# Keys and queries loaded once, both heads' scores side by side on 64 rows, one transfer to turn the results

## The chip, the core and the metric

The kernel runs on one core of a Trainium2 chip. The metric is the device time of one execution in microseconds (us). Before the change three runs took 953.39, 953.75 and 956.28 us, median 953.75. The engines are named as in the profile: PE (matrix products; PEld is its weight load), DVE (vector), ACT (scalar), POOL (GpSimd), and SP, which here only issues transfers (DMA).

## What is computed

Attention with a window and global keys, then a two-layer MLP with the Mish function, on its output read as tokens. `d` is 64, there are 8 batches and 8 heads, 512 local and 32 global positions, and the MLP maps 4608 tokens of 512 to 2048 and back.

```python
s_g = scale * q_g @ [k_g, k_l]^T                  # 32 global queries see all 544 keys
out_g = softmax(s_g) @ [v_g, v_l]
s_l = scale * [q_l @ k_g^T, q_l @ k_l^T where |i - j| <= 32]
out_l = softmax(s_l) @ [v_g, v_l]
x = concat([out_g, out_l]) as (4608, 512) tokens
h = x @ w_in                                      # (512, 2048)
g = h * tanh(softplus(h))
return g @ w_out                                  # (2048, 512)
```

## The kernel before, in words

**Tiles.** Two heads form a head pair, and a batch `b` has four of them (`hp`). A head pair's 512 local queries are four tiles `t` of 128. A tile sees a window of 192 or 224 key columns, in which the 32 global keys stand (`WIN`). One (b, hp, t) is a *unit*; there are 128. The tokens of a batch make two MLP blocks of 256, and the global tokens of all batches a seventeenth. A block passes eight *steps*: each step takes 256 of the 2048 hidden columns through `m1_mm` (product `h`, line 915), `mish` (ACT, line 958), `g_hi`/`g_lo` (split into two fp16 parts) and `m2_mm` (product `o`, line 983).

**Precision.** An fp32 operand is split into a high part and a remainder, both fp16, and a product is made of three fp16 products (high by high, high by low, low by high). The weights come in 64-bit words, which DVE takes apart (`w_bits`, `w_sum`) slice by slice, before a statistic over the whole matrix (`w_stat` on PE, `w_norm`, line 463) gives the scale with which `w_split` splits them. So the first `h` needs all of the first matrix, and the first `o` all of the second.

**Scores.** For the first eight head pairs (batches 0 and 1, `plain_s`) scores are fp32 products over 64 rows, one per head, line 692. For the other 24 the keys and queries lie twice in a tile of 128 rows: both row halves of `kraw` and of `qraw` hold the same head's 64 numbers, the two heads one behind the other in the columns. `q_hi` writes the high part over all 128 rows of `qs`, `q_lo` puts the remainder over its upper 64, `k_hi` and `k_lo` make `ks` and `kl`. One product of `qs` by `ks` over 128 rows thus holds two of the terms, and a second by `kl` the third (line 699). Each tile and head has a PSUM bank of its own from the ring "sc" of three, read by `row_max` (DVE, line 705); `expo` (ACT, line 714) follows, then `p_hi`, `p_lo` (`ph`), a DMA transpose into `pt`, and `pv` (product `U`, line 783). `g_scores` (line 823) does the global queries with 32 columns of weights for each head, its two parts in two more banks of "sc".

**Results.** `x_norm` divides, `x_split` makes two fp16 parts in `xs`, and `x_turn` turns them with two DMA transposes into `xh` and `xl`, from which `m1_mm` reads. In batch 0 PE turns `pt` and `x` instead.

**Order.** Nothing is issued as it is written. `Plan.add` records each piece of work with what it reads and writes, an engine (or two to choose from) and a cost in ns; `Plan.order` is a list scheduler over these costs, and `emit` writes the engines' instructions in its order. Each engine runs them in that order, and all transfers go through SP. `slot(u)` is the order of priority in which pieces are added for unit u; `ORDER`, `CONV1` and the other constants set where the first loads and the work on the weights come. In the stretch before PE has enough to do, the planner adds *fillers*: products of a constant into `w_s` (line 1211) that nothing reads.

Of the kernel before, what the change touches and what calls it, by code (L numbers as in the profile page):

```python
# [39 lines left out]
NPS = 8  # L40
# [11 lines left out]
class Plan:  # L52
# [10 lines left out]
    SLACK = 357.177  # L63
    TARGET = 6095.107
    SPARE_T = 129630.527
    BOOST = 0.15
    SPARE = 1463.76
    TABLE = 1283

    def __init__(self):  # L70
        self.tasks = []
        self.rings = {}
        self.count = {}
        self.last = {}
# [7 lines left out]
        self.fill, self.filler = {}, None  # L82

# [17 lines left out]
    def add(self, eng, ns, fn, r=(), w=(), new=(), pri=0, rows=1.0, table=None):  # L101
# [14 lines left out]
        for tag, name in new:  # L116
            bufs, make = self.rings[tag]
            k = (tag, self.count[tag] % bufs)
            self.count[tag] += 1
            for wr, rd in self.state.get(k, {}).values():  # L120
                deps |= rd
                if wr is not None:
                    deps.add(wr)
# [5 lines left out]
            self.state[k] = {None: (n, set())}  # L129
        for x in w:  # L130
            k, sub = self._key(x)
            st = self.state.setdefault(k, {})
            for s, (wr, rd) in st.items():
# [112 lines left out]
def attn_mish_kernel(ctx: ExitStack, tc: tile.TileContext, qt, kt, qt0, kt0, mxs, vm, vg, qg, w1, w2, consts_in, out, w64):  # L246
# [23 lines left out]
    def rings(pool, *table):  # L270
        for tag, bufs, shape, dt in table:
# [5 lines left out]
          ("vraw", 1, [128, HP, 4, 128], F32), ("vgraw", 1, [128, 128], F32), ("qgraw", 1, [128, 3, HP, 64], F32),  # L277
# [14 lines left out]
          ("xh", 2, [128, HP, SL], F16), ("xl", 2, [128, HP, SL], F16),  # L292
# [32 lines left out]
    def dma(kib):  # L325
        return 410, kib * 3.05
# [4 lines left out]
    def dma_on(kib):  # L331
        return 590, 250 + kib * 4.5
# [52 lines left out]
    PLACE = dict(zip(range(16), ["xh", "xl"] * 2 + list(range(9, 18)) + ["G"] * 3))  # L385
    PLACE.update(zip(range(16, 32), ["G"] * 3 + [17, 16, 15, 14, "kraw", "qraw", "ob", 17, 16, "kraw", "qraw", "ob", 8]))

    def raw(k):
# [13 lines left out]
    def w_load(k):  # L402
# [11 lines left out]
        if w64:  # L414
            p = PLACE[k]
            pl.add(DMA, bulk(512), go, w=[rawkey(k)] if p in range(18) else (), new=() if p in range(18) else [(p, ("wraw", k))])
# [175 lines left out]
    def g_split(b):  # L592

        q, rq, sk = ("qgh", b), ("qgraw", b), ("sk", b)
        pl.add([(ACT, act(512, 1)), (DVE, dve2(512, 1))], 0, lambda e: scaled(e, X[q], X[rq][:, 1:3], X[sk][:, 0:1]), r=[rq, sk], new=[("qgh", q)])
        for a, h in ((0, HI), (1, LO)):
            pl.add(DVE, dve(256, 1), lambda a=a, h=h: V.scalar_tensor_tensor(X[q][h, a], X[rq][h, 1 + a], X[sk][h, 0:1], X[q][h, a], ALU.mult,
                                                                          ALU.subtract), r=[rq, sk], w=[[q, a]])
# [22 lines left out]
    def q_hi(b, hp):  # L621
        q, qs = ("qraw", b, hp), ("qs", b, hp)
        pl.add(COPY(1024, b), 0, lambda e: scaled(e, X[qs], X[q], X["sk", b][:, 0:1]), r=[q, ("sk", b)], new=[("qs", qs)])

    def q_lo(b, hp):

        q, qs = ("qraw", b, hp), ("qs", b, hp)
        pl.add(DVE, dve(1024, 1) + 90, lambda: V.scalar_tensor_tensor(X[qs][HI], X[q][HI], X["sk", b][HI, 0:1], X[qs][HI], ALU.mult, ALU.subtract),
               r=[q, ("sk", b)], w=[qs])

    def k_hi(b, hp):
        k, ks = ("kraw", b, hp), ("ks", b, hp)
        pl.add(COPY(1280, b), 0, lambda e: scaled(e, X[ks], X[k], X["sk", b][:, 1:2]), r=[k, ("sk", b)], new=[("ks", ks)])

    def k_lo(b, hp, h):
        k, ks, kl = ("kraw", b, hp), ("ks", b, hp), ("kl", b, hp)
        pl.add(DVE, dve(640, 1), lambda: V.scalar_tensor_tensor(X[kl][:, h], X[k][:, h], X["sk", b][:, 1:2], X[ks][:, h], ALU.mult, ALU.subtract),  # L637
               r=[k, ks, ("sk", b)], w=[[kl, h]], new=() if h else [("kl", kl)])
# [46 lines left out]
    def scores(b, hp, t, h):  # L685
        qs, ks, kl, s = ("qs", b, hp), ("ks", b, hp), ("kl", b, hp), ("s", b, hp, t, h)
        c0, w, m0 = WIN[t]
        r = slice(h * 64, h * 64 + 64)

        if plain_s(b, hp):  # L690
            (q, part), (k, _) = pair(b, hp, "qn"), pair(b, hp, "kn")
            pl.add(PE, mm(1, 4 * w) + 50, lambda: T.matmul(X[s][:, :w], X[q][r, part, t * 128:(t + 1) * 128],
# [605 lines left out]
```

## Time and profile before

| | us |
|---|---|
| runs, median | 953.75 |
| profiled execution, device time | 956.89 |
| its span, first to last instruction | 955.1 |
| ACT busy | 640.0 |
| read from HBM | 75.15 MB |
| granted TensorE clock, mean | 0.985 |

An engine's busy time is the union of its instructions, and a matmul's row shows it from its start to the modelled end, so that rows of matmuls overlap: what one costs is the distance between starts. `x103` counts instructions. A row of waits gives the idle time in total, how often, and the longest. The views that the prediction rests on are shown there.

### The profile page before, as it was taken

Reading aid. Unit: us, or ns where it says so; the run is one execution under the profiler, and the core shown is the slowest. Engines: PE = TensorE matmul, PEld = TensorE weight load, DVE = VectorE, ACT = ScalarE, POOL = GpSimd, SP = SyncE. Lnnn points to the kernel's source line nnn. Section 1 sums busy time; section 2 is a strip of 40 time slices with the busy share of each in tenths; the row PEclk is TensorE's granted clock in tenths of the full one; section 3 lists DMA queues with packets and bytes.
Section 4 is the critical chain, followed back from the end, with each engine's and each line's share of the span. In section 5 each row is a group of like instructions: output and inputs, shape, how many; then the busy total and the mean of one; then the engine's idle time right before and its main releaser. Section 6 shows DMA issues by size and latency. Waiting matters only on the chain.

```text
span 955.1 us, 20897 instructions
## 1 busy us (share of the span) xinstructions
PE 919.5 (96%) x8115; PEld 634.9 (66%) x8115; DVE 665.5 (70%) x1775; ACT 640.0 (67%) x1293; POOL 17.6 (2%) x28
## 2 busy tenths in 40 slices
PE   7899999999999999999999999999999999999995
PEld 4566765567676676777767676767777766666663
DVE  6799989779899898767766777768777552322221
ACT  4577778697767889978877887788868771212110
POOL 2000000000000000000000000000000000000000
PEclk8899999999999999999999999999999999999998
DMA  9877458987999896758585676567764430000000
GB/s 303 283 242 234 164 135 204 171 218 193 218 216 255 217 261 150 163 130 185 130 166 118 166 157 148 117 155 166 157 124 102 81 74 12 23 1 23 4 20 22
DMA packets 214011, 141.02 MB, mean 148 GB/s; under 512 B 176664, under 2 KB 188184, under 8 KB 212888
## 3 DMA queue, kind: packets, MB, share of 16 engines
q1 hardware_dynamic: 213912, 139.69, 60.3%
q8 instruction: 63, 1.03, 0.5%
q14 instruction: 36, 0.29, 0.1%
HBM read 75.15 MB, written 8.91 MB: 88 GB/s over the span
## 4 chain that ended last, share of the span: by engine, by line
PE 61%; DVE 19%; ACT 8%; DMA 6%; issue 4%; SPq 1%; POOL 0%; DVEq 0%; ACTq 0%
PE o L983 26%; PE h L915 26%; PE U L783 3%; DMA pt<-ph 2%; PE s L699 2%; DVE G L971 2%; DVE P L705 2%; ACT P L714 2%; ACT L958 2%; DMA vraw<-in_vm 2%; PE g L823 1%; DVE G L351 1%; DVE W L430 1%; ACT e L958 1%; DMA W<-in_w 1%
## 5 line engine op out<-in xcount | busy, mean ns | idle before, releaser
L983 PE MATMUL o<-W,G 128*128 128x512 f16 x1632 | 391.7, 380 | 3.4 <-ACT ob L349 1.3
L915 PE MATMUL h<-xh,W 128*128 128x256 f16 x2048 | 375.9, 273 | 0.9 <-ACT e L958 0.8
L915 PEld LDWEIGHTS <-W 128*128 128x128 f16 x3264 | 311.2, 98 | 66.5 <-issue 6.5
L915 PE MATMUL h<-xl,W 128*128 128x256 f16 x1024 | 279.1, 273 | 0.0
L983 PEld LDWEIGHTS <-G 128*128 128x128 f16 x1632 | 156.8, 98 | 149.3 <-issue 7.7
L958 ACT ACTIVATE e<-h,c 128x512 f32<-128x512 f32 (+1 forms) x137 | 91.5, 682 | 123.8 <-PE h L915 118.4
L351 DVE TENSOR_SCALAR G<-e,c 128x512 f16<-128x512 f32 (+1 forms) x122 | 58.5, 481 | 151.5 <-ACT e L958 151.3
L714 ACT ACTIVATE P<-P,nm 128x192 f32<-128x192 f32 (+1 forms) x256 | 118.0, 461 | 55.1 <-DVE nm L705 52.6
L766 DVE SCALAR_TENSOR_TENSOR ph<-P,ph 128x384 f16<-128x384 f32 (+1 forms) x112 | 65.0, 582 | 57.9 <-ACT ph L349 57.4
L971 DVE SCALAR_TENSOR_TENSOR G<-e,c,G 128x512 f16<-128x512 f32 (+1 forms) x137 | 101.8, 744 | 2.7
L705 DVE CUSTOM_DVE_ANT_0 P<-s,consts 128x192 f32<-128x192 f32 (+1 forms) x256 | 90.9, 362 | 18.2 <-PE s L699 11.4
L958 ACT ACT_TABLE_LOAD x64 | 82.1, 1283 | 1.1
L714 ACT ACT_TABLE_LOAD x60 | 77.0, 1283 | 1.5 <-DVE nm L705 0.4
L783 PEld LDWEIGHTS <-pt 96*128 96x128 f16 (+1 forms) x1536 | 61.5, 98 | 13.2 <-DMA pt<-ph 6.4
L349 ACT ACTIVATE ph<-P 128x384 f16<-128x384 f32 (+1 forms) x111 | 60.2, 547 | 11.8 <-DMA pt<-ph 9.6
L783 PE MATMUL U<-va,pt 128*128 128x64 f16 (+1 forms) x768 | 55.3, 193 | 3.9 <-DMA pt<-ph 3.7
L783 PE MATMUL U<-vc,pt 96*128 96x64 f16 x768 | 55.2, 193 | 0.0
L699 PEld LDWEIGHTS <-qs 128*128 128x128 f16 x384 | 35.3, 98 | 20.7 <-issue 3.4
L714 ACT ACTIVATION_READ_ACCUMULATOR P<-P,nm 128x1 f32 x256 | 47.9, 187 | 0.0
L699 PE MATMUL s<-ks,qs 128*128 128x192 f16 (+1 forms) x192 | 42.6, 253 | 1.5 <-ACT gP L845 0.7
L699 PE MATMUL s<-kl,qs 128*128 128x192 f16 (+1 forms) x192 | 42.5, 252 | 0.0
L637 DVE SCALAR_TENSOR_TENSOR kl<-kraw,sk,ks 128x640 f16<-128x640 f32 x48 | 41.6, 867 | 0.0
(132 smaller groups left out, 935.6 us busy)
## 6 DMA issues: line engine op xcount, KB each, us to landing
kraw<-in_kt SPq DMA_DIRECT2D x24, 640.0 KB, 4.8
kn_m<-in_mxs SPq DMA_DIRECT2D x24, 544.0 KB, 4.8
qraw<-in_qt SPq DMA_DIRECT2D x24, 512.0 KB, 3.4
out<-ob SPq DMA_DIRECT2D x34, 256.0 KB, 2.5
vraw<-in_vm SPq DMA_DIRECT2D x8, 1024.0 KB, 5.9
wraw<-in_w SPq DMA_DIRECT2D x16, 512.0 KB, 6.2
W<-in_w SPq DMA_DIRECT2D x16, 512.0 KB, 5.8
vc<-vf SPq DMA_DIRECT2D x32, 128.0 KB, 2.4
```

The source lines that it names most:

```text
L349: A.activation(out=dst, in_=src, func=AF.Copy, scale=c)
L351: V.tensor_scalar(dst, src, c, None, ALU.mult)
L637: pl.add(DVE, dve(640, 1), lambda: V.scalar_tensor_tensor(X[kl][:, h], X[k][:, h], X["sk", b][:, 1:2], X[ks][:, h], ALU.mult, ALU.subtract ...
L699: T.matmul(X[s][:, :w], X[qs][:, h, t * 128:(t + 1) * 128], X[k][:, h, c0:c0 + w], start=(i == 0), stop=(i == 1))
L705: pl.add(DVE, 69 + 1.04 * w, lambda: V.tensor_tensor_reduce(out=X[P][:, h, :w], in0=X[s][:, :w], in1=mask[:, m0:m0 + w], scale=-SCALE, sca ...
L714: pl.add(ACT, 94 + 0.832 * w + 186, lambda: A.activation(out=X[P][:, h, :w], in_=X[P][:, h, :w], func=AF.Exp, bias=X[nm], scale=-1.0, accu ...
L766: pl.add(DVE, dve(n), lambda: V.scalar_tensor_tensor(p_part(X[ph], t, 1), p_src(X[P], t), PSC, p_part(X[ph], t, 0), ALU.mult, ALU.subtract ...
L783: T.matmul(X[u][:, t, h, :], X[pt][:k, p * 4 + h * 2 + c, :], X[vx][:k, t, vl, h * 64:(h + 1) * 64], start=(n == 0), stop=(n == 5))
L915: T.matmul(X[h][:, f * TB:(f + 1) * TB], wh(i, wl)[:, off:off + 128], X[x][:, d, o:o + TB], start=(n == 0), stop=(n == 11))
L958: chain(blk, i, ACT, 587, lambda a, z: A.activation(out=X[e][:, a:z], in_=hv(blk, i)[:, a:z], func=AF.Mish, bias=0.0, scale=X[c][:, 0:1]), ...
L971: chain(blk, i, DVE, 663, lambda a, z: V.scalar_tensor_tensor(gp(1, blk, i)[:, a:z], X[e][:, a:z], X["c", blk][:, 2:3], gp(0, blk, i)[:, a ...
L983: T.matmul(X[o], gp(g, blk, i)[:, f, t * 128:(t + 1) * 128], wh(8 + i, wl)[:, f * 512:(f + 1) * 512], start=(i == 0 and n == 0), stop=(i = ...
```

## The change

**Loads.** Keys and queries lie once in memory and in SBUF: 64 rows of one head and 64 of the other. One transfer brings two head pairs; the fp32 batches read the same arrays. The rows of global queries shrink as well (`qgraw`, 128x320 instead of 128x768).

**Splits.** `qs` now has a high part and a remainder side by side in columns, `ks` and `kl` are 640 columns wide instead of 1280.

**Scores.** One piece of work makes the scores of both heads of two tiles, in two banks of "sc", 64 rows for each head, head after head: three terms in fp16, one in fp32. `g_scores` takes 128 columns of weights, in which the other heads' places multiply rows by zeros or give rows that are not read.

**Results.** `xh` and `xl` become `xx`, and one transpose fills both parts; staged weights lie two to a buffer there. The planner tracks writes to parts of a buffer for that. Its costs for transfers and its constants are changed.

```diff
-    SLACK = 357.177
-    TARGET = 6095.107
-    SPARE_T = 129630.527
-    BOOST = 0.15
-    SPARE = 1463.76
+    SLACK = 452.499
+    TARGET = 3424.086
+    SPARE_T = 56888.29
+    BOOST = 0.706
+    SPARE = 914.873
...
-          ("qs", 2, [128, 2, SL], F16), ("ks", 2, [128, 2, KW], F16), ("kl", 2, [128, 2, KW], F16), ("qgh", 2, [128, 2, HP, 64], F16),
+          ("qs", 2, [128, 2, SL], F16), ("ks", 2, [128, KW], F16), ("kl", 2, [128, KW], F16), ("qgh", 2, [128, 2, HP + 1, 64], F16),
...
-          ("xh", 2, [128, HP, SL], F16), ("xl", 2, [128, HP, SL], F16),
+          ("xx", 2, [128, HP, 2, SL], F16),
...
     def k_load(b, hp):
-        pl.add(DMA, dma(640), lambda: load(X["kraw", b, hp], kt[b, hp]), new=[("kraw", ("kraw", b, hp))])
+        n = b * HP + hp
+        pl.add(DMA, dma(640), lambda: load(X["kraw", b, hp // 2], kt[n:n + 2].rearrange("a p n -> p a n")), new=[("kraw", ("kraw", b, hp // 2))])
...
-        pl.add(DVE, dve(1024, 1) + 90, lambda: V.scalar_tensor_tensor(X[qs][HI], X[q][HI], X["sk", b][HI, 0:1], X[qs][HI], ALU.mult, ALU.subtract),
+        pl.add(DVE, dve(512, 1), lambda: V.scalar_tensor_tensor(X[qs][:, 1], X[q][:, hp % 2], X["sk", b][:, 0:1], X[qs][:, 0], ALU.mult, ALU.subtract),
...
-    def scores(b, hp, t, h):
-        qs, ks, kl, s = ("qs", b, hp), ("ks", b, hp), ("kl", b, hp), ("s", b, hp, t, h)
-        c0, w, m0 = WIN[t]
-        r = slice(h * 64, h * 64 + 64)
+    def scores(b, hp, t):
+        s = [("s", b, hp, t // 2, h) for h in range(2)]
+        new = [("sc", x) for x in s]
+        ts = (t, t + 1)
+
+        def products(terms):
+            for u in ts:
+                c0, w, m0 = WIN[u]
+                c = slice(u % 2 * 256, u % 2 * 256 + w)
+                for i, (q, k) in enumerate(terms):
+                    for h, r in enumerate((LO, HI)):
+                        T.matmul(X[s[h]][:, c], q[r, u * 128:(u + 1) * 128], k[r, c0:c0 + w], start=(i == 0), stop=(i == len(terms) - 1))
...
-        def go():
-            for i, k in enumerate((ks, kl)):
-                T.matmul(X[s][:, :w], X[qs][:, h, t * 128:(t + 1) * 128], X[k][:, h, c0:c0 + w], start=(i == 0), stop=(i == 1))
-        pl.add(PE, mm(2, w + 10), go, r=[qs, ks, [kl, h]], new=[("sc", s)])
+        pl.add(PE, sum(3 * (WIN[u][1] / 2.4 + 7) for u in ts) + 200, lambda: products(
+            [(X[qs][:, 0], X[ks]), (X[qs][:, 0], X[kl]), (X[qs][:, 1], X[ks])]), r=[qs, ks, kl], new=new, rows=0.6)
...
     def x_turn(b, hp, t):
...
-        for i, x in enumerate((("xh", b), ("xl", b))):
-            turn(32 * n, lambda x=x: X[x][:, hp, cols].rearrange("p (t q) -> p t q", t=n),
...
+        xs, xx = ("xs", b, hp), ("xx", b)
+        turn(256, lambda: X[xx][:, hp].rearrange("p a (t q) -> p (a t) q", t=4), lambda: X[xs].rearrange("p a t c -> p (a t c)"), r=[xs],
+             w=[[xx, (hp, half)] for half in range(2)], new=() if hp else [("xx", xx)])
...
-        pl.add(PE, mm(2, 262) + 90 + (1 - part) * 62, lambda: products(*(
-            (h * 32, h * 32 + 32, [(X[q][:, h, hp, h * 32:h * 32 + 32], X[k][:, h]) for k in (ks, kl)]) for h in range(2))),
+        two = lambda n: X[q][:, n, hp:hp + 2, :].rearrange("p a q -> p (a q)")
+        pl.add(PE, mm(3, 262) + (1 - part) * 45, lambda: products(128, [(two(0), X[ks]), (two(1), X[ks]), (two(0), X[kl])]),
...
-        if fu:
-            att(scores, *fu, 0)
-            att(scores, *fu, 1)
+        if fu and fu[2] % 2 == 0:
+            att(scores, *fu)
...
-    ORDER = "k0 q0 m b q1 w0 w1 k1 g w3 w2 k2 w5 q2 w6 w4 w7 k3 w8 q3 w12 w14 w9 w13 w11 w10 w15"
+    ORDER = "k0 q0 m w1 k1 q1 g w3 b k2 w0 w2 w5 q2 w6 w7 w4 w8 k3 w15 w12 w14 q3 w11 w9 w13 w10"
```

What this makes of the order. On PE, where scores are fp16, before issues for one tile (here tile 2 of head pair 2) first one head and then the other; `s_2_2_0` is head 0 and `s_2_2_1` head 1, `ks` and `kl` the key parts, `o` the product ahead.

```order
L983 MATMUL o_1_7945<-W,G_7713 128x512
L699 LDWEIGHTS qs_2_7372
L699 MATMUL s_2_2_0_8018<-ks_2_7425,qs_2_7372 128x224
L699 LDWEIGHTS qs_2_7372
L699 MATMUL s_2_2_0_8018<-kl_2_7435,qs_2_7372 128x224
L699 LDWEIGHTS qs_2_7372
L699 MATMUL s_2_2_1_8021<-ks_2_7425,qs_2_7372 128x224
```

The change, same engine and part, at the first tile of a pair (`s_2_0_0` and `s_2_0_1` are the heads' banks for tiles 0 and 1 of head pair 2):

```order
L934 MATMUL h_2_7821<-xx_6093,W 128x256
L715 LDWEIGHTS qs_2_7305
L715 MATMUL s_2_0_0_7838<-ks_2_7415,qs_2_7305 128x192
L715 LDWEIGHTS qs_2_7305
L715 MATMUL s_2_0_1_7839<-ks_2_7415,qs_2_7305 128x192
L715 LDWEIGHTS qs_2_7305
L715 MATMUL s_2_0_0_7838<-kl_2_7418,qs_2_7305 128x192
```

The heads alternate, each with its own weights, and twelve products stand in a row for two tiles where four stood for one. Over the whole program the fp16 score products go from 384 to 576, the products of `g_scores` in fp16 from 288 to 216, the fillers from 103 to 176, and the `h` products ahead of the first `o` from 216 to 240.

On ACT, in the same part, before comes back to its Mish table for each unit or two (`e` is Mish, `P` the exponentials of `expo`, whose name carries head pair, tile and head):

```order
L958 ACT_TABLE_LOAD
L958 ACTIVATE e_3_7335<-h_3_7199,c_5723 128x512
L958 ACTIVATE e_4_7345<-h_4_7291,c_5723 128x512
L349 ACTIVATE qs_2_7372<-qraw_2_7045,sk_4862 128x1024
L714 ACT_TABLE_LOAD
L714 ACTIVATE P_77,sums_0_7121<-P_77,nm_0_3_0_7370 128x192
L714 ACTIVATE P_77,sums_0_7121<-P_77,nm_0_3_1_7390 128x192
L349 ACTIVATE ph_82<-P_77 128x2x192
```

The change at the same units:

```order
L739 ACT_TABLE_LOAD
L739 ACTIVATE P_76,sums_0_7135<-P_76,nm_0_2_0_7288 128x224
L739 ACTIVATE P_76,sums_0_7135<-P_76,nm_0_2_1_7307 128x224
L739 ACTIVATE P_77,sums_0_7135<-P_77,nm_0_3_0_7310 128x192
L739 ACTIVATE P_77,sums_0_7135<-P_77,nm_0_3_1_7327 128x192
L358 ACTIVATE ph_81<-P_76 128x2x224
```

Tiles 2 and 3 now follow each other under one table. ACT's order holds 129 table loads before and 111 now.

On DVE, at the program's start, before begins with the row maxima (`P,nm` from `s`):

```order
L1219 TENSOR_SCALAR nid<-consts 128x128
L705 ISA P_75,nm_0_0_0_118<-s_0_0_0_111,consts 128x192
L705 ISA nm_0_0_0_118 128x1
L705 ISA P_75,nm_0_0_1_124<-s_0_0_1_116,consts 128x192
L705 ISA nm_0_0_1_124 128x1
```

and the change with a slice of the weights (`W` from `wraw`):

```order
L1234 TENSOR_SCALAR nid<-consts 128x128
L444 TENSOR_SCALAR W<-wraw_100 128x512
L446 SCALAR_TENSOR_TENSOR W<-wraw_100,W 128x512
L730 ISA P_75,nm_0_0_0_122<-s_0_0_0_108,consts 128x192
L730 ISA nm_0_0_0_122 128x1
L453 SCALAR_TENSOR_TENSOR W<-wraw_100,W 128x512
```

The slice moved ahead of the row maxima, and its load, on SP, ahead of the load of `vraw`.

More of the change, by code (lines that the diff above doesn't have):

```diff
@@ L119, in add @@
             self.count[tag] += 1
+            old = set(self.base.get(k, set()))
             for wr, rd in self.state.get(k, {}).values():
-                deps |= rd
+                old |= rd
                 if wr is not None:
-                    deps.add(wr)
+                    old.add(wr)
+            deps |= old
+            part = any(isinstance(x, list) and x[0] == name for x in w)
+            self.base[k], self.alloc[k] = (old, {n}) if part else (set(), set())
             if tag in self.last:
@@ L128, in add @@
             self.owner[k] = name
-            self.state[k] = {None: (n, set())}
+            self.state[k] = {None: (None if part else n, set())}
         for x in w:
@@ L415, in w_load @@
             p = PLACE[k]
-            pl.add(DMA, bulk(512), go, w=[rawkey(k)] if p in range(18) else (), new=() if p in range(18) else [(p, ("wraw", k))])
+            new = p not in range(18) and wname(k) not in pl.place
+            pl.add(DMA, bulk(512), go, w=[rawkey(k)] if not new or p == "xx" else (), new=[(p, wname(k))] if new else ())
         else:
@@ L594, in g_split @@
         q, rq, sk = ("qgh", b), ("qgraw", b), ("sk", b)
[L595 to L598, printed above, removed]
+        pl.add([(ACT, act(320, 1)), (DVE, dve2(320, 1))], 0, lambda e: scaled(e, X[q][:, 0], X[rq], X[sk][:, 0:1]), r=[rq, sk], new=[("qgh", q)])
+        pl.add(DVE, dve(320, 1), lambda: V.scalar_tensor_tensor(X[q][:, 1], X[rq], X[sk][:, 0:1], X[q][:, 0], ALU.mult, ALU.subtract),
+               r=[rq, sk], w=[q])
     def b_split(b):
@@ L690, in scores @@
         if plain_s(b, hp):
             (q, part), (k, _) = pair(b, hp, "qn"), pair(b, hp, "kn")
-            pl.add(PE, mm(1, 4 * w) + 50, lambda: T.matmul(X[s][:, :w], X[q][r, part, t * 128:(t + 1) * 128],
-                                                      X[k][r, part, c0:c0 + w], start=True, stop=True),
-                   r=[[q, part], [k, part]], new=[("sc", s)], rows=0.25)
+            pl.add(PE, sum(250 + 1.4375 * WIN[u][1] for u in ts) + 100, lambda: products([(X[q][:, part], X[k][:, part])]),
+                   r=[[q, part], [k, part]], new=new, rows=0.25)
@@ L804, in x_turn @@
     def x_turn(b, hp, t):
-        g, ts = group(b, hp, t)
-        xs, q, cols, n = ("xs", *g), slice(ts[0], ts[-1] + 1), slice(ts[0] * 128, ts[-1] * 128 + 128), len(ts)
-        first = hp == 0 and ts[0] == 0
-        for i, x in enumerate((("xh", b), ("xl", b))):
-            turn(32 * n, lambda x=x: X[x][:, hp, cols].rearrange("p (t q) -> p t q", t=n),
-                 lambda i=i: X[xs][:, i, q].rearrange("p t c -> p (t c)"), r=[xs],
-                 w=[[x, (hp, half)] for half in range(2) if 2 * half in ts], new=[(x[0], x)] if first else ())
+        xs, xx = ("xs", b, hp), ("xx", b)
@@ L1062, in slot @@
             k_hi(*n2)
[L1063 to L1066 removed]
+            k_lo(*n2)
         if more1 and t == 1:
```

178 lines of the change are left out of this document (88 added, 90 removed).

## The prediction

> **What bounds the kernel now.** I read the engines' busy time first, then the same in seven stretches, then the waits of the engine that is busiest.
>
> ```profile
> PE 919.5 (96%) x8115; PEld 634.9 (66%) x8115; DVE 665.5 (70%) x1775; ACT 640.0 (67%) x1293; POOL 17.6 (2%) x28
> ```
>
> The TensorE (PE) has work 96% of the time. An average says little about a change that touches DVE, ACT and the loads as well, so here is the split by stage (stretch, its length, then busy time of PE, weight loads, DVE, ACT, POOL, then granted clock, DMA share and GB/s).
>
> ```profile
> 0.00:60.00 60.00, 47.55 (x386) 31.73 (x387) 44.75 (x132) 30.94 (x83) 6.79 (x13) 0.86 0.89 291
> 60.00:130.00 70.00, 66.07 (x560) 46.66 (x557) 66.84 (x189) 54.13 (x121) 1.73 (x3) 1.00 0.64 195
> 130.00:217.00 87.00, 84.55 (x728) 51.50 (x728) 73.62 (x187) 69.52 (x140) 1.64 (x2) 0.98 0.80 181
> 217.00:318.00 101.00, 97.94 (x967) 70.35 (x965) 94.38 (x251) 75.90 (x169) 2.35 (x4) 1.00 0.91 219
> 318.00:420.00 102.00, 100.94 (x963) 71.70 (x962) 82.82 (x222) 86.81 (x166) 1.70 (x2) 1.00 0.80 190
> 420.00:776.00 356.00, 353.84 (x3332) 250.16 (x3331) 255.57 (x708) 288.08 (x565) 3.36 (x4) 1.00 0.64 138
> 776.00:945.00 169.00, 168.62 (x1194) 112.79 (x1190) 47.05 (x91) 34.60 (x56) 0.00 (x0) 1.00 0.06 19
> ```
>
> Three regimes. Up to 130 us DVE leads: it works 66.84 of 70 us from 60 to 130, and PE's high share there includes filler products (the 103 matmuls of line 1211 below), which compute nothing that is stored. From 130 to 776 us PE has work for all but 2.45 + 3.06 + 1.06 + 2.16 = 8.7 us. From 776 to 945 only the two weight products are left, idle 0.4 us. So whatever an edit takes from DVE, ACT or the DMA queues after 130 us is worth at most a part of 8.7 us; what it adds to or takes from PE there counts in full; and the time of the first m2 product (o, line 983) says how long the start is.
>
> ```profile
> L983 PE MATMUL o<-W,G x1632: 376/379/634, 129.6 to 944.2; 128*128 128x512 f16 x182
> ```
> ```profile
> L1211 PE MATMUL w_s<-consts x103: 270/273/421, 7.2 to 113.2; 128*128 128x256 bf16 x103
> ```
> ```profile
> L463 DVE CUSTOM_DVE_ANT_0 wd<-w_s,consts x2: 282/287/292, 59.8 to 118.3; 128x128 f32<-128x128 f32 x2
> ```
>
> The first o starts at 129.6 us and the last at 944.2. It waits for the scale of the second weight matrix, whose statistic DVE reduces at 118.3 (second of line 463); the fillers lie ahead of that (7.2 to 113.2).
>
> **The change part by part, against the profiled execution's own 956.9 us.**
>
> *Scores of heads in fp16 (24 head pairs, 48 pairs of query tiles).* Before, a tile takes four products over 128 rows:
>
> ```profile
> 448.84 0.25 PE L699 MATMUL s<-ks,qs 128*128 128x192 f16 x1
> 448.92 0.25 PE L699 MATMUL s<-kl,qs 128*128 128x192 f16 x1
> 449.00 0.25 PE L699 MATMUL s<-ks,qs 128*128 128x192 f16 x1
> 449.08 0.25 PE L699 MATMUL s<-kl,qs 128*128 128x192 f16 x1
> 449.17 0.25 PE L783 MATMUL U<-va,pt 128*128 128x64 f16 x3
> 449.25 0.26 PE L783 MATMUL U<-vc,pt 96*128 96x64 f16 x3
> ```
> ```profile
> 442.89 0.26 PE L699 MATMUL s<-ks,qs 128*128 128x224 f16 x1
> ...
> 443.27 0.25 PE L783 MATMUL U<-va,pt 96*128 96x64 f16 x3
> ```
>
> Starts are 0.08 us apart at 192 columns (449.17 - 448.84 = 0.33 us for the tile) and 0.095 at 224 (443.27 - 442.89 = 0.38), so a pair of tiles costs 0.71 us. The column rate is 0.42 ns, which makes 0.080 and 0.093 us of pure streaming. After, a pair of tiles is six passes, each with both heads on 64 rows side by side: 3 x 0.080 + 3 x 0.093 = 0.52 us, if nothing else is added. The f32 scores of the first two batches already run on 64 rows, and show what is added:
>
> ```profile
> 143.54 0.25 PE L783 MATMUL U<-vc,pt 96*128 96x64 f16 x3
> 143.72 0.59 PE L692 MATMUL s<-kn,qn 64*128 64x192 f32 x4
> 144.25 0.26 PE L783 MATMUL U<-va,pt 128*128 128x64 f16 x3
> ```
> ```profile
> 154.50 0.65 PE L692 MATMUL s<-kn,qn 64*128 64x224 f32 x4
> 155.08 0.60 PE L983 MATMUL o<-W,G 128*128 128x512 f16 x2
> ```
>
> Three U products take 0.09 us (449.17 to 449.25), yet s starts 0.18 after the last three: 0.09 us to enter. s to the next row is 0.53 at 192 columns and 0.58 at 224; the 0.05 for 32 more columns in two passes means 0.8 ns a column, 0.16 us a pass, so 0.21 us of the 0.53 is not streaming but the first weights and the way back. So a visit to the 64-row shape costs 0.30 us, 0.09 before it and 0.21 behind. In fp16 the first weights should be cheaper (a U product with its own weights takes 0.03 us), so I put a visit at 0.09 + 0.09 + 0.04 = 0.22 us, and a pair of tiles at 0.52 + 0.22 + 0.01 = 0.75: 0.04 more than the 0.71 before. **48 x 0.04 = +2 us** (bounds +1 with weights at 0.03, +5 with the whole 0.30). Fewer columns are streamed, and the visit eats it.
>
> The Trainium skill, "TensorEngine Tiling (Array Packing)", Key Properties, says that a change of tiling mode drains the TensorE; the 0.09 us ahead of s agrees. Its table Theoretical Speedup promises up to 2x for a 64-row product; six passes instead of eight without any drain would make this term 48 x (0.52 - 0.71) = -9 us, and the rows above speak against it.
>
> *Global queries' scores.* Before, two heads on 32 columns each:
>
> ```profile
> 450.73 0.27 PE L915 MATMUL h<-xh,W 128*128 128x256 f16 x1
> 450.93 0.29 PE L823 MATMUL g<-ks,qgh 128*32 128x256 f16 x2
> ...
> 451.53 0.28 PE L915 MATMUL h<-xh,W 128*128 128x256 f16 x1
> ```
>
> An h product takes 0.11 us (it starts 0.11 before the next one), so entering costs 0.09 here too, and the visit ends 0.60 after g starts: 0.69 us. After: nine full-shape products, six of 256 columns and three of 32: 6 x 0.11 + 3 x 0.03 = 0.75, and no change of shape. Where before made two visits out of its two parts it paid some 0.2 more. 24 x (+0.06 to -0.15): **0** (+1.5 to -3.5).
>
> *f32 scores, second batch.* Two tiles become one visit: 8 pairs x 0.30 = -2.4 us behind 130 us. Also, before split heads in places, and a head alone costs what two cost:
>
> ```profile
> 152.22 0.59 PE L692 MATMUL s<-kn,qn 64*128 64x192 f32 x2
> 152.74 0.60 PE L983 MATMUL o<-W,G 128*128 128x512 f16 x2
> ```
>
> 0.52 us for one head (0.53 for both above); two such splits less, -1. **-3.4 us** (0 to -4).
>
> *Order.* After runs 240 h products ahead of its first o instead of 216, in a time in which PE waits for weights anyway: 24 x 0.11 = **-2.6 us** of work taken from behind 130 us (0 to -2.6). The 73 added fillers also lie ahead of it; at 0.11 us they are 8 us in a stage that DVE bounds, and cost nothing as long as PE has that room.
>
> *DVE, ACT, loads.* Rows of what shrinks:
>
> ```profile
> L958 ACT ACT_TABLE_LOAD x64 | 82.1, 1283 | 1.1
> ...
> L637 DVE SCALAR_TENSOR_TENSOR kl<-kraw,sk,ks 128x640 f16<-128x640 f32 x48 | 41.6, 867 | 0.0
> ...
> L628 DVE SCALAR_TENSOR_TENSOR qs<-qraw,sk,qs 64x1024 f16<-64x1024 f32 x24 | 30.8, 1285 | 0.8
> ```
>
> kl: 24 of 867 ns less, -21 us. q's remainder: 24 of 1285 ns over 1024 columns become 24 over 512, some 700 ns by kl's 867 over 640, -14 us. The first halves shrink likewise on either engine. ACT loads its tables 18 times less (111 instead of 129 in its order), 18 x 1.283 = -23 us, since two units' exponentials now follow each other. The 48 loads of k and q (640 and 512 KB) become 24 of the same sizes, 24 x 0.576 = 14 MB less to read, and those of the global queries shrink to 160 KB; 28 of the 56 transposes of results go, and the merged one is as large as the transposes of ph. All this is beside PE's work. It can only shorten the 8.7 us of idle PE behind 130 us, whose largest part is
>
> ```profile
> PE U L783 <- DMA pt<-ph: 3.7, 5, 1.1
> ```
>
> a transpose that comes late behind DVE, ACT and the queue. DVE works 94.38 of 101 us between 217 and 318, so there it helps. I take 40%: **-3.5 us** (0 to -8.7). A new wait is added for the bank: two tiles of both heads take two of the three "sc" banks until the second tile's row maximum is read, one unit later; the next pair's scores, the g parts and PE behind them wait for it, if DVE is late. At a DVE that is 72% busy (255.57 of 356) I expect none. The one buffer of k is now held until the second head pair is split, and the next load then has two units' work of PE ahead of its use, against the time that one takes to land:
>
> ```profile
> kraw<-in_kt SPq DMA_DIRECT2D x24, 640.0 KB, 4.8
> ```
>
> Two units hold two MLP steps, 48 h products at 0.11 us alone 5.3, so the 4.8 us stay covered; without that cover each of the 12 loads could cost up to 4.8 us.
>
> *The start.* Up to 130 us the longest of DVE's waits, but for the first constants, are these:
>
> ```profile
> DVE P L705 <- PE s L692: 4.2, 5, 1.6
> DVE W L428 <- DMA W<-in_w: 2.9, 1, 2.9
> ```
>
> The new order fetches a weight slice ahead of vraw, and DVE converts it before the first row maxima; that fills some of both waits. Its other constants are a new draw: -6 to +6 us, I take **-1**.
>
> Sum: 2 + 0 - 3.4 - 2.6 - 3.5 - 1 = -8.5 us: 948.4 against 956.9. The median shown is 953.75, 3.1 below the profiled execution; the same difference gives 945.3.
>
> **The rivals.**
>
> *Hidden anyway.* PE is already full behind 130 us and the visits cost what they save; the idle time and the start stay. Then 2 + 0 - 2.4 is left, 953.75 - 0.4 = 953.4. For it: 353.84 of 356 us busy. Against it: the f32 splits and the 24 products are countable.
>
> *Slower: weights in the 64-row shape are not hidden.* Each of six passes brings new weights for the same rows. If each exposes what the first does, 0.21 - 0.09 = 0.12 us by the f32 rows, five more passes cost 48 x 5 x 0.12 = +29 us, and 945.3 becomes 974. The gain of the other terms is used up (10.5 us over 48 pairs, 0.22 us each) once a pass costs 0.04 more than streaming, some 0.125 us. Against it: the second f32 pass shows no such gap, as two passes and one 0.21 fill the 0.53. For it: an f32 pass is 0.16 us long and covers a load that an fp16 pass of 0.08 may not. The Trainium skill, "TensorE: Matmul & The Clock Gate", The mechanism, states that LDWEIGHTS overlaps matmuls in flight only when their row group differs; by that rule this rival holds, and the f32 rows don't agree with it.
>
> *The start slips.* DVE orders its 0 to 118 us anew; if the second reduction of line 463 comes 10 us later, everything does: the -1 becomes +10, 956 or more.
>
> *The middle closes.* All of the 8.7 us goes and the start gains 6: 945.3 - 5.2 - 5 = 935.
>
> **How the numbers follow.** The forecast (936 to 951) 0.60; hidden anyway 0.16; weights exposed 0.07; the start slips 0.12 (to 965); the middle closes, below 936, 0.05. Predicted 945.3. The range 935 to 960 leaves out the weights, most of the lower tail and the worst starts, 0.16 in all. 0.3%, about what a measurement can tell from no change, is 2.9 us: faster is below 950.9 with 0.65, same 0.16, slower above 956.6 with 0.19.
>
> **What would show it.** In the changed profile: a pair's s rows from first to next row near 0.66 us, and 0.09 ahead of them (1.2 us or more: weights exposed, or heads one after the other); the first o at 126 to 131 us; ACT_TABLE_LOAD down by 18; PE idle between the first o and the last s at 4 to 7 us. I am wrong if the first o moves by more than 5 us, or if PE waits for the "sc" banks.

## The result, and the profile after

The changed kernel takes 945.51 us, median of seven runs (942.76 to 948.66); the kernel before took 953.39 beside it (seven runs, 949.95 to 956.28). The ratio is 0.9922 (95% interval 0.9898 to 0.9947). The forecast was 945.3, range 935 to 960. The profiled execution of the changed kernel took 948.66 us, its span is 946.9; against the 956.9 of the kernel before that is -8.2, where the sum gave -8.5.

The total agrees better than its terms do. First the page after, the engines' busy time.

```profile
PE 913.5 (96%) x8308; PEld 631.9 (67%) x8308; DVE 643.2 (68%) x1776; ACT 582.8 (62%) x1244; POOL 16.2 (2%) x28
```

ACT is relieved of 57 us and DVE of 22, PE of 6. The same seven stretches as before (columns as there):

```profile
0.00:60.00 60.00, 46.74 (x416) 33.81 (x417) 47.41 (x144) 33.36 (x92) 6.79 (x13) 0.93 0.90 297
60.00:130.00 70.00, 66.57 (x620) 50.39 (x618) 64.99 (x174) 50.70 (x111) 1.80 (x3) 0.99 0.59 176
130.00:217.00 87.00, 83.82 (x781) 52.61 (x779) 74.12 (x208) 70.50 (x148) 2.52 (x2) 1.00 0.86 176
217.00:318.00 101.00, 98.12 (x975) 68.19 (x976) 86.48 (x240) 84.64 (x180) 2.08 (x4) 1.00 0.95 214
318.00:420.00 102.00, 102.00 (x989) 71.52 (x988) 77.54 (x216) 70.77 (x151) 1.14 (x2) 1.00 0.59 138
420.00:776.00 356.00, 356.00 (x3425) 248.72 (x3424) 250.02 (x721) 244.13 (x522) 1.86 (x4) 1.00 0.55 116
776.00:936.00 160.00, 160.00 (x1113) 106.67 (x1110) 41.88 (x75) 28.42 (x43) 0.00 (x0) 1.00 0.05 15
```

From 318 us on PE is never without work; between 130 and 318 it still lacks 3.2 + 2.9 us. The rows of `o` and of the weights' statistic, by line:

```profile
L1002 PE MATMUL o<-W,G x1632: 376/379/390, 131.7 to 935.9; 128*128 128x512 f16 x182
```
```profile
L479 DVE CUSTOM_DVE_ANT_0 wd<-w_s,consts x2: 273/278/283, 66.6 to 119.5; 128x128 f32<-128x128 f32 x2
```

The first `o` starts 2.1 us later than before (131.7 against 129.6), the last 8.4 earlier (935.86 against 944.25). So the gain, 10.5 us, lies wholly between the first `o` and the last. To see what made it I took the trace's time from each product's start to the next one's, added it up by what the product writes, and counted what exceeds the usual 0.109 us (`h`), 0.217 (`o`) and 0.031 (`U` and global `U`) ahead of a score product as the price of entering that score:

| between first and last `o`, us | before | after | difference | forecast |
|---|---|---|---|---|
| fp16 scores, with entering | 36.40 | 35.34 | -1.1 | +2 |
| f32 scores, with entering | 7.66 | 5.21 | -2.4 | -3.4 |
| global scores, with entering | 21.05 | 21.80 | +0.7 | 0 |
| `h` (3048 products, then 3024) | 333.70 | 331.12 | -2.6 | -2.6 |
| PE idle | 8.78 | 6.06 | -2.7 | -3.5 |
| `o` (1631) | 354.57 | 353.11 | -1.5 | none |
| `U` and global `U` | 52.51 | 51.52 | -1.0 | none |
| together | 814.68 | 804.16 | -10.5 | -7.5 |
| first `o` | 129.6 | 131.7 | +2.1 | -1 |

The timeline of the changed kernel at a pair of fp16 tiles (start, length, engine, line; a row of `x2` is both heads):

```profile
450.64 0.26 PE L715 MATMUL s<-ks,qs 64*128 64x192 f16 x2
450.74 0.25 PE L715 MATMUL s<-kl,qs 64*128 64x192 f16 x2
450.82 0.34 PE L715 MATMUL s<-ks,qs 64*128 64x192 f16 x4
451.00 0.26 PE L715 MATMUL s<-kl,qs 64*128 64x224 f16 x2
451.10 0.26 PE L715 MATMUL s<-ks,qs 64*128 64x224 f16 x2
451.29 0.26 PE L808 MATMUL U<-va,pt 128*128 128x64 f16 x3
```

Six passes 0.08 to 0.10 us apart and a gap of 0.19 behind the last (0.095 of streaming, the rest the way back): 0.64 us in each of the 48 pairs, and 0.095 to enter. That is 0.737 us against the forecast's 0.75. No fp16 pair waits for a bank. Yet the term came out 3 us better than forecast, mostly because *before* was worse than the rows that I had quoted. This is the kernel before at one of its visits (PE and ACT):

```profile
581.11 0.25 PE L699 MATMUL s<-ks,qs 128*128 128x192 f16 x1
...
581.20 0.25 PE L699 MATMUL s<-kl,qs 128*128 128x192 f16 x1
581.23 0.19 ACT L845 ACTIVATION_READ_ACCUMULATOR gP<-g,gmx 64x1 f32 x1
...
581.47 0.24 PE L699 MATMUL s<-ks,qs 128*128 128x192 f16 x1
...
581.63 0.25 PE L783 MATMUL U<-va,pt 128*128 128x64 f16 x3
```

The second head starts 0.27 us after the first head's last product, not 0.08, just after ACT's exponentials have left a bank of the ring "sc" (0.19 us from 581.23): the global queries' part was still in it. Nine visits between 272 and 732 us show such a hole, 0.17 to 0.5 us long, 2.8 us together; eight end with ACT's `gP`, the first with DVE's row maximum (`nm`). In the view of waits less than half of this is seen, since a matmul's modelled end is 0.25 us behind its start and only what exceeds that counts as idle:

```profile
PE s L699 <- ACT gP L845: 0.7, 3, 0.2
PE s L699 <- DVE nm L705: 0.6, 2, 0.4
```

So about 1.5 us of the holes stand in the row of the fp16 scores, and the other 1.3 in the row of idle time.

### The profile page after: what moved, and what is told of

It reads as the page before. It is cut to its first block, busy times and chain, and to the rows that moved or that the text cites. A ratio compares the mean times of both kernels' runs of the same rounds, so it can differ in the third digit from the quotient of the medians.

```text
span 946.9 us, 21111 instructions
## 1 busy us (share of the span) xinstructions
PE 913.5 (96%) x8308; PEld 631.9 (67%) x8308; DVE 643.2 (68%) x1776; ACT 582.8 (62%) x1244; POOL 16.2 (2%) x28
## 4 chain that ended last, share of the span: by engine, by line
PE 81%; DVE 7%; DMA 7%; ACT 2%; issue 0%; SPq 0%; POOL 0%; ACTq 0%
PE h L934 34%; PE o L1002 34%; DMA pt<-ph 4%; PE U L808 4%; PE s L715 3%; PE g L842 2%; DMA wraw<-in_w 1%; DMA W<-in_w 1%; PE gu L891 1%; DVE W L446 1%; DVE W L453 1%; DVE P L730 1%; DVE W L508 1%; DVE W L444 1%; DVE vmx L555 1%; PE w_l L515 0%
## 5 line engine op out<-in xcount | busy, mean ns | idle before, releaser
L1002 PE MATMUL o<-W,G 128*128 128x512 f16 x1632 | 380.0, 379 | 0.9 <-DVE W L508 0.9
L934 PE MATMUL h<-xx,W 128*128 128x256 f16 x3072 | 363.8, 273 | 0.1
L977 ACT ACTIVATE e<-h,c 128x512 f32<-128x512 f32 (+1 forms) x137 | 93.5, 684 | 200.5 <-PE h L934 178.9
L730 DVE CUSTOM_DVE_ANT_0 P<-s,consts 128x192 f32<-128x192 f32 (+1 forms) x256 | 87.8, 362 | 4.0 <-PE s L715 4.0
L358 ACT ACTIVATE ph<-P 128x448 f16<-128x448 f32 (+1 forms) x99 | 51.3, 542 | 9.8 <-DMA pt<-ph 9.1
L668 DVE SCALAR_TENSOR_TENSOR vf<-vraw,sv,vf 128x512 f16<-128x512 f32 x32 | 23.9, 748 | 16.4 <-ACT vf L358 16.4
L856 DVE TENSOR_REDUCE gmx<-g 64x1 f32<-64x288 f32 x64 | 25.7, 427 | 13.3 <-PE g L842 13.3
L715 PE MATMUL s<-ks,qs 64*128 64x192 f16 (+1 forms) x384 | 34.0, 252 | 0.0
L864 ACT ACTIVATE gP<-g,gmx 64x288 f32<-64x288 f32 x64 | 30.2, 475 | 5.2 <-DVE gmx L859 3.7
L585 DVE TENSOR_REDUCE mx<-kn_m 128x1 f32<-128x1088 f32 x24 | 30.5, 1276 | 3.0 <-DMA kn_m<-in_mxs 2.8
```

What stands on the lines that cost most here:

```text
L358: A.activation(out=dst, in_=src, func=AF.Copy, scale=c)
L585: pl.add(DVE, dve(1088), lambda i=i, k=k: V.tensor_reduce(out=X[mx][:, i:i + 1], in_=X[k].rearrange("p a n -> p (a n)")[:, :1088], axis=AX ...
L715: T.matmul(X[s[h]][:, c], q[r, u * 128:(u + 1) * 128], k[r, c0:c0 + w], start=(i == 0), stop=(i == len(terms) - 1))
L730: pl.add(DVE, 69 + 1.04 * w, lambda: V.tensor_tensor_reduce(out=X[P][:, h, :w], in0=X[s][:, c], in1=mask[:, m0:m0 + w], scale=-SCALE, scal ...
L934: T.matmul(X[h][:, f * TB:(f + 1) * TB], wh(i, wl)[:, off:off + 128], X[xx][:, d, x, o:o + TB], start=(n == 0), stop=(n == 11))
L977: chain(blk, i, ACT, 587, lambda a, z: A.activation(out=X[e][:, a:z], in_=hv(blk, i)[:, a:z], func=AF.Mish, bias=0.0, scale=X[c][:, 0:1]), ...
```

## Experiments

Unless it is said, the order of the work is the changed kernel's: an edit is unknown to the planner. Ratios are to the kernel before, timed beside each run. Its medians there were 951.56 us (30 runs) for heads apart, two visits, two transposes and no fillers; 951.37 (17) for work done twice; 953.2 (7) for the constants; 952.2 (17) for the f32 visits and for the loads that the planner knows of.

### Must the heads alternate?

```diff
-                for i, (q, k) in enumerate(terms):
-                    for h, r in enumerate((LO, HI)):
+                for h, r in enumerate((LO, HI)):
+                    for i, (q, k) in enumerate(terms):
```

> The changed kernel, but within a visit to the 64-row shape all products of one head come first and then all of the other (same products, same planner, same order of everything else). If the two heads really run side by side only because they alternate, an fp16 pair of tiles goes from six passes to almost twelve, 0.52 us more, 48 times: +25 us, and the f32 pairs behind 130 us some +5: about 975. If PE overlaps the heads in any order of issue, or if they were never side by side: 945.

The edit acts within each tile: three products of one head, then three of the other. 945.83 us, 0.9944 (0.9927 to 0.9961). The trace shows why it costs nothing:

```profile
451.67 0.26 PE L715 MATMUL s<-ks,qs 64*128 64x192 f16 x2
451.76 0.25 PE L715 MATMUL s<-kl,qs 64*128 64x192 f16 x2
451.84 0.35 PE L715 MATMUL s<-ks,qs 64*128 64x192 f16 x4
452.02 0.27 PE L715 MATMUL s<-kl,qs 64*128 64x224 f16 x2
452.12 0.27 PE L715 MATMUL s<-ks,qs 64*128 64x224 f16 x2
452.32 0.26 PE L808 MATMUL U<-va,pt 128*128 128x64 f16 x3
```

A row still has two products: the second head's first one starts 10 ns after the first head's first, ahead of the first head's second. The pair takes 0.648 us from first to next, against 0.642. As its order is the changed kernel's and its time the same within the intervals, this run stands in for the changed kernel below, where it was timed beside the others.

### Does a visit to the 64-row shape cost what the sum says?

```diff
+                if len(terms) == 3 and u == t:
+                    q, k = terms[0]
+                    T.matmul(X[s[0]][:, 480:512], q[:, 0:128], k[:, 0:32], start=True, stop=True)
```

> The changed kernel with one product of 32 columns over all 128 rows put between the two tiles of an fp16 pair, into columns that nothing reads: two visits to the 64-row shape instead of one. By the price of a visit in the profile of the changed kernel (0.09 ahead and 0.64 - 0.52 = 0.12 behind, with 0.03 for the product itself) 48 x 0.24 = +11.5 us: 957. If the change of shape costs nothing by itself, only the product counts: 48 x 0.03 = +1.5: 947.

955.99 us, 1.0038 (1.0021 to 1.0055): 10.2 us above the run with heads apart, 48 x 0.21.

```profile
754.19 0.26 PE L715 MATMUL s<-ks,qs 64*128 64x192 f16 x2
754.28 0.25 PE L715 MATMUL s<-kl,qs 64*128 64x192 f16 x2
754.36 0.24 PE L715 MATMUL s<-ks,qs 64*128 64x192 f16 x2
754.54 0.19 PE L718 MATMUL s<-ks,qs 128*128 128x32 f16 x1
754.66 0.27 PE L715 MATMUL s<-ks,qs 64*128 64x224 f16 x2
...
754.86 0.26 PE L715 MATMUL s<-ks,qs 64*128 64x224 f16 x2
755.05 0.39 PE L937 MATMUL h<-xx,W 128*128 128x256 f16 x2
```

The pair now takes 0.87 us from first to next (mean of 48), 0.23 more with the product between; scores between the first and the last `o` rise by 11.0. Without some 0.03 for the product itself, the second visit costs 0.20 us, close to the 0.22 of the forecast. The same in the eight f32 pairs of the second batch, with a product of the constants between the tiles:

```diff
+                if len(terms) == 1 and b == 1 and u == t:
+                    T.matmul(X[s[0]][:, 480:512], ident.bitcast(BF16)[:, :128], ident.bitcast(BF16)[:, :32], start=True, stop=True)
```

> The changed kernel; in the eight pairs of tiles of the second batch, whose scores are in f32, one product of 32 columns over 128 rows stands between the two tiles (into columns of the scores' bank that nothing reads), so that a pair takes two visits to the 64-row shape again. The order of everything else is the same. If a visit costs the 0.30 us of the prediction, 8 x 0.30 = 2.4 us and the product itself some 0.03 each: about +2.6 us, 0.9950 of the kernel before (946.7 to 948), and a pair's s rows run 1.2 us from first to next instead of 0.906. If the f32 shape overlaps its changes as it does its second pass, +0.5 us or less: 0.993 and the pair stays below 1.0 us.

946.91 us, 0.9937 (0.9916 to 0.9957): the interval holds both forecasts, the trace decides.

```profile
133.32 0.65 PE L715 MATMUL s<-kn,qn 64*128 64x224 f32 x4
133.90 0.19 PE L717 MATMUL s<-consts 128*128 128x32 bf16 x1
134.02 0.59 PE L715 MATMUL s<-kn,qn 64*128 64x192 f32 x4
134.55 0.39 PE L1004 MATMUL o<-W,G 128*128 128x512 f16 x1
```

134.55 - 133.32 = 1.23 us where the changed kernel takes 0.906: 0.32 more with the extra product, so some 0.30 for a visit. But only five of the eight pairs lie behind the first `o`; the others pass in the start, where they cost nothing.

### Is the merged transfer beside PE's work?

```diff
-        turn(256, lambda: X[xx][:, hp].rearrange("p a (t q) -> p (a t) q", t=4), lambda: X[xs].rearrange("p a t c -> p (a t c)"), r=[xs],
...
+            for a in range(2):
+                nc.sync.dma_start_transpose(X[xx][:, hp, a].rearrange("p (t q) -> p t q", t=4), X[xs][:, a].rearrange("p t c -> p (t c)"))
```

> The changed kernel with the results of a head pair turned by two transposes of half the size again, into the same tile. If the merged transpose is beside the path, as the sum had it: 945 to 946.5. If it was part of the gain (28 transposes less on the queue ahead of those of ph): +2 us or more, and longer waits of the h products.

952.77 us, 1.0003 (0.9981 to 1.0025): 6.9 us above the run with heads apart. "Beside the path" has fallen. PE is idle 13.7 us between the first and the last `o` instead of 6.1 (7.3 in the run with heads apart), and the wait that grew is not that of the `h` products but that for the transposes of `ph`. Here the waits of this run, and then of the changed kernel:

```profile
PE U L808 <- DMA pt<-ph: 9.4, 9, 2.3
```
```profile
PE U L808 <- DMA pt<-ph: 3.1, 5, 1.1
```

Why: the transposes of results on SP (minimum, median, maximum in ns), of this run and of the changed kernel.

```profile
L834 SPq DMA_TRANSPOSE xx<-xs x56: 1188/1217/1893, 148.5 to 788.2; - x56
```
```profile
L541 SPq DMA_TRANSPOSE xx<-xs x28: 1231/1236/2754, 151.0 to 781.7; - x28
```

One of half the size holds SP for 1.217 us, the whole one for 1.236. Two in place of one keep the only queue for 1.2 us more, 28 times, and the next transpose of `ph` stands behind them. (The planner was given the cost of one, so this is the price with an order that does not make room.)

### Did the lighter DVE, ACT and loads make the gain?

Three runs do parts of the old work over again, a fourth all three: DVE computes `kl` and the queries' remainder twice (its busy time 678.4 us instead of 643.2), ACT copies `ob` and the high part of `v` twice (623.5 instead of 582.8), or keys and queries are loaded twice, the second time into a tile that nothing reads (24 issues and 14 MB more). One line of each:

```diff
-        pl.add(DVE, dve(640, 1), lambda: V.scalar_tensor_tensor(X[kl], X[k][:, hp % 2], X["sk", b][:, 1:2], X[ks], ALU.mult, ALU.subtract),
+        pl.add(DVE, dve(640, 1), lambda: [V.scalar_tensor_tensor(X[kl], X[k][:, hp % 2], X["sk", b][:, 1:2], X[ks], ALU.mult, ALU.subtract) for _ in range(2)],
...
-            pl.add(engs, 0, lambda e, t=t, o=o: scaled(e, X[ob][:, t], X[o], X[c][:, 1:2]), r=[o, [c, 1]], w=[[ob, t]],
+            pl.add(engs, 0, lambda e, t=t, o=o: [scaled(e, X[ob][:, t], X[o], X[c][:, 1:2]) for _ in range(1 + (e == ACT))], r=[o, [c, 1]], w=[[ob, t]],
...
-        pl.add(DMA, dma(640), lambda: load(X["kraw", b, hp // 2], kt[n:n + 2].rearrange("a p n -> p a n")), new=[("kraw", ("kraw", b, hp // 2))])
+        pl.add(DMA, dma(640), lambda: [load(x, kt[n:n + 2].rearrange("a p n -> p a n")) for x in (X["kraw", b, hp // 2], junk)], new=[("kraw", ("kraw", b, hp // 2))])
```

> The changed kernel with each of the 24 kl and 24 qs remainders computed twice on DVE (24 x 0.87 + 24 x 0.75 = 39 us by their rows in the changed kernel), unknown to the planner, so the order stays: DVE's load is that of before again. If the lighter DVE is worth at most the idle PE that went away behind 217 us (3.4 us): 945.5 to 948. If DVE's relief made the gain: +6 us or more.

> The changed kernel with the copies of the results (ob) and the high parts of v on ACT done twice, some 33 x 0.68 + 27 x 0.72 = 42 us of ACT, about what it lost in work and table loads; order unchanged. If ACT's relief is worth at most part of the 3.4 us: 945.5 to 948. If it made the gain: +6 us or more.

> The changed kernel with each load of keys and queries done twice, the second time into a tile that nothing reads: 24 loads and 14 MB more, as before. If the smaller loads are hidden: 945.5 to 946.5. If the queues' load made the transposes of ph late: U products wait longer and +2 us or more.

> The changed kernel with the extra work of the last three runs all together: DVE, ACT and the queues as full as before, PE's work and order as in the change. If relief is worth the 3.4 us of idle PE behind 217 us: 947 to 950, with that idle time back. If the gain is PE's own work and its order alone: 945.5. If relief is the whole gain: 953.

| work done twice | us | ratio | PE idle, first to last `o` |
|---|---|---|---|
| DVE | 951.0 | 0.9994 (0.9984 to 1.0005) | 8.3 |
| ACT | 958.18 | 1.0069 (1.0057 to 1.0081) | 13.4 |
| loads | 966.17 | 1.0149 (1.0132 to 1.0166) | 18.7 |
| all three | 979.5 | 1.0297 (1.0279 to 1.0314) | 30.0 |

None of it is hidden: they lie 7 (with both intervals, 4 to 9), 14, 22 and 36 us above the 0.9922 of the changed kernel, and all but the first are slower than the kernel before. What waits differs. ACT's extra work comes ahead of what frees the banks of `o`; the loads keep the transposes of `ph` back. Rows of waits of the ACT run, then of the run with loads, and SP's timeline of the latter:

```profile
PE o L1002 <- ACT ob L358: 6.1, 9, 2.2
```
```profile
PE U L809 <- DMA pt<-ph: 15.5, 8, 4.6
```
```profile
288.38 0.47 SPq L348 DMA_DIRECT2D junk<-in_kt  x1
288.89 0.47 SPq L348 DMA_DIRECT2D qraw<-in_qt  x1
293.70 0.37 SPq L348 DMA_DIRECT2D junk<-in_qt  x1
...
296.18 6.65 SPq L542 DMA_TRANSPOSE pt<-ph  x2
```

The two transposes are not what is longer here. In the changed kernel the same two, behind their single loads, hold SP just as long, though 1.27 us is the median of one:

```profile
282.25 6.73 SPq L541 DMA_TRANSPOSE pt<-ph  x2
```

They start late. From 289.4 to 293.7 us SP stands still: the second copies go into one tile, `junk`, so that of the queries waits until that of the keys has landed (293.63), and all transfers behind it wait too. SP's waits for this copy ahead of a load:

```profile
SPq L348 <- DMA junk<-in_kt: 13.1, 3, 4.6
```

PE's 4.6 us of waiting ends at 304.6 us, behind this stall, and two more of its four longest waits (2.1 us at 174.3, 3.2 us at 246.4) come behind the other two. Each of the four longest waits has 3.4 us at half the granted clock close behind it (from 155.0, 175.5, 247.2 and 305.2 us), by estimate 4 x 1.7 = 7 us more; the changed kernel has none of these stretches. In the kernel before each load of keys or queries has a tile of its own, so a part of the 22 us, and of the 36, is the price of this experiment's own tile and not of the loads; no run separates the two. So PE's idle time of 6 us does not say that the other engines have room: each engine's order is fixed, and work that it does not know of delays whatever stands behind it, at the same place every time. That is no measure of what the relief was worth to the kernel before, though, whose order was drawn for its heavier load. The fair form of the question is to tell the planner what the loads take, those of the queries in the same way (512 to 1024):

```diff
-        pl.add(DMA, dma(640), lambda: [load(x, kt[n:n + 2].rearrange("a p n -> p a n")) for x in (X["kraw", b, hp // 2], junk)], new=[("kraw", ("kraw", b, hp // 2))])
+        pl.add(DMA, dma(1280), lambda: [load(x, kt[n:n + 2].rearrange("a p n -> p a n")) for x in (X["kraw", b, hp // 2], junk)], new=[("kraw", ("kraw", b, hp // 2))])
```

> The changed kernel with the 24 loads of keys and queries done twice (14 MB more read, the second copy into a tile that nothing reads), as in the run with its loads back, but here the planner is told that each takes twice as long on the queue, and so draws its order with it. If that run lost 22 us because the order did not know of the loads, most of it comes back: 945 to 953 us. If the loads themselves stand in the way of the transposes of ph whatever the order, 958 to 967. If any newly drawn order is worse with constants that were chosen for another, as where the constants were exchanged, it can also lie above 967, and then the waits of PE are not those for the transposes of ph alone.

With its own order, 950.16 us, 0.9972 (0.9955 to 0.9988): 17 us of the 22 are back. What is left is 0.9972 - 0.9922, some 5 us (with both intervals, 2 to 8). PE idles 10.7 us, and:

```profile
PE U L809 <- DMA pt<-ph: 6.9, 11, 1.2
```

the waits for `pt` are shorter and more of them. Here too the second copy waits for the first in two places (6.5 us of SP), and the constants were chosen for another order. So 5 us is what the doubled loads cost in this form; how much of the gain the halved loads made is not shown.

### Is it the change, or its constants? (a new order)

The 23 constants change places, in each of the two kernels; a few of them, in the changed one:

```diff
-    LEAD0 = 18.538
-    PACE = 0.697
+    LEAD0 = 13.22
+    PACE = 0.728
...
-    CONV1 = 2.35
-    RATE1 = 0.451
+    CONV1 = 9.424
+    RATE1 = 1.041
```

> The changed kernel with the 23 scheduling constants of before (order of the first loads, slots of the weights' work, pace, filler settings); loads, splits, scores and transposes stay changed. By the sum, where the constants were worth -1 and the 24 more h products ahead of the first o -2.6: 947 to 950. If the new constants are the whole gain: 953 or more. If they are worth nothing, or lost the 2 us of the start: 943 to 946.

> The kernel before with the 23 scheduling constants of the change, nothing else. If the constants alone bring the gain: 946. If they only fit the changed kernel's work: 953 or slower. By the sum, -3.6 of the -8.5 at the most: 950 to 953.

The change with the constants of before: 973.54 us, 1.0195 (1.0162 to 1.0228). Before with the constants of the change: 962.05, 1.0088 (1.0054 to 1.0122). Each is slower than either kernel with its own constants, by far more than was expected of the first. Rows of `o` in the two:

```profile
L1002 PE MATMUL o<-W,G x1632: 376/379/391, 148.8 to 958.0; 128*128 128x512 f16 x182
```
```profile
L983 PE MATMUL o<-W,G x1632: 376/379/632, 120.2 to 948.9; 128*128 128x512 f16 x182
```

In the first the start loses 17 us (148.8 against 131.7; 288 `h` products lie ahead of the first `o`, not 240), in the second the first `o` comes 9 us *earlier* than before and the end still 5 later: only 72 of the `h` products lie ahead of it instead of 216, and 144 x 0.11 = 16 us of them move behind it. This also bears out the order term: a product counts only on which side of the first `o` it lies, and an early first `o` is no gain by itself. Neither set of constants fits the other kernel, so the -0.8% is that of edits and constants together; no run separates them.

### Do the fillers cost anything?

```diff
-                self.filler[2]()
+                pass
```

> The changed kernel with none of its 176 filler products; everything else stands in the same order. If the fillers only fill idle PE and their number costs nothing, but they hold the clock: the granted clock in the first 130 us falls, DVE waits longer for s products, first o later by 2 to 6 us: 947 to 952. If they stand in the way of the start (the first o was 2 us later than before): first o earlier, 943 or less.

948.32 us, 0.9969 (0.9956 to 0.9982): without all 176 the kernel is 2.5 us slower than the run with heads apart, whose interval just overlaps. So the fillers together cost nothing; the 73 added ones alone were not taken out. Why they help is not settled. The ten executions without them have granted clocks from 0.987 to 0.997, six of them at 0.990 or below; the nine of the run with heads apart lie from 0.990 to 0.995. That points to the clock, but the execution that was profiled is one of the shorter ones (span 945.3, clock 0.996) and shows no loss.

## Why the prediction was right

**The fp16 scores** were forecast at +2 and came out at -1.1. The price of a visit, 0.22 us, was nearly right (0.20, measured by doubling it), and so were the pair, 0.737 for 0.75, and the rejection of the rival of exposed weights: new weights for the same rows every 0.08 to 0.10 us leave no hole. One reading behind that rejection was off, though. The two passes of an f32 visit start 0.267 us apart at 192 columns, not 0.16, so a gap of 0.10 does stand ahead of the second pass; it is the third and fourth passes of the changed kernel's f32 pairs, 0.16 us at 192 columns, that have none. By the rule of the Trainium skill, "TensorE: Matmul & The Clock Gate", The mechanism, that weights overlap only where the row group differs, the pair would have cost by estimate 0.6 us more (five passes at the rival's 0.12); these rows don't agree with it. The same section also names a background buffer for weights, into which they can be loaded ahead; with that these rows agree. The mis-sized part is the 0.71 us of *before*: its rows were taken from undisturbed visits, and the mean over all 48 pairs is 36.40 / 48 = 0.758, with about 1.5 us of the waits for the third bank in the 36.40. A gain that I had not seen: two banks for a pair, and no hole in any of 48.

**f32 scores**: -2.4 for -3.4. The visit's 0.30 was right (0.32 with the extra product), the count was not: five pairs behind the first `o`, not eight. With 5 x 0.30 = 1.5 the two split tiles, 0.5 each, make up the rest.

**Global scores**: +0.7 for 0, within the bounds: nine products take 0.73 us, before 0.69 with entering, 24 x 0.04 = 1.

**Order**: -2.6 as forecast, 24 `h` products less behind the first `o`; some `U` products moved with them, -1.0.

**DVE, ACT, loads**: idle time fell by 2.7 where I took 3.5 of 8.7. The size is about right, the mechanism is not. The largest part, PE's wait for the transposes of `ph`, hardly moved (3.7 to 3.1 us). Of what went, 1.5 us are the waits of the fp16 scores for a bank, which belong to the scores and not to a lighter engine; 1.3 us are waits for `ob` and 0.8 for Mish, both ACT's, and new waits of about 1.5 us came in. Nor does "all this is beside PE's work" hold for the merged transfer, whose undoing costs 6.9 us with the order held; for the loads it is open. The limit of 8.7 us held between two kernels whose orders each fit their load; it is no limit on what undoing a single piece costs, and the pieces add up to more than the whole.

**The start**: +2.1 for -1, inside its bounds. It is hardly a finding: with the same order up to there, the first `o` of the profiled runs above (the first eight and the f32 one) starts between 129.2 and 132.5 us.

**Not in the sum**: -1.5 us in `o` with equally many products. The kernel before ran at half the granted clock from 131.8 to 135.2 us, just behind its first `o` (its longest `o` took 634 ns, after 390); in the changed profile such stretches lie at 20 to 27 and 58 to 61 us only, in the start. The other profiled execution of that kernel's work, with the new constants, has one too (121.2 to 124.6 us, behind its first `o` at 120.2); the changed kernel and the seven runs that keep its order without doubled loads have none between their first and last `o`. Whether the change makes it rarer, or these executions happened so, is open.

Of the signs named in advance, the pair's 0.66 (0.64), the 0.09 ahead of it, idle time of 4 to 7 us (6.06), and 18 table loads less held. No fp16 score waits for a bank of "sc"; behind the first `o` only one f32 global product waits 0.3 us for a row maximum. The first `o` missed its 126 to 131 by 0.7.

So the agreement of 945.5 with 945.3 is in part luck: what lies between first and last `o` was 3 us better than forecast, the start 3 us worse.

## What to carry to other kernels

Price an instruction of the kernel before from all of its occurrences: a wait shorter than a matmul's modelled end is in no view of idle time, only in the distance between starts. Where a planner fixes each engine's order, a bound from idle time holds only for work that the planner knows of; adding unknown work to an engine with a third of its time free cost a fifth to a third of what it took. An experiment that adds work must not add a wait of its own: two spare copies into one tile stopped the only queue three times. And count transfers, not only bytes: on a queue that one engine issues, a transpose half as large took the same 1.2 us.

## What the runs showed of the hardware

Two heads on separate 64 rows run side by side whether their products are issued in turn or one head after the other (0.642 and 0.648 us for a pair); the starts of the two heads are 3 and 10 ns apart. A change to the 64-row shape and back costs about 0.2 us in fp16 (0.095 ahead and about 0.11 more than streaming in the visit) and about 0.30 in f32. A DMA transpose occupies SP for 1.2 us whether it turns one part or two, and two of `ph` behind loads held it for 6.7 us. Each of the four PE waits of 2 to 4.6 us in the run with loads was followed by 3.4 us at half the granted clock; the two of 2.2 and 2.3 us in the run with two transposes were not.
